# Sorting the eighth pair of heads as well: its rows ranked and scattered while early pairs are computed

## The chip, the cores and the metric

The kernel runs on one core of one Trainium2 chip. Its engines are TensorE (PE in the profile, with its weight loads as PEld), VectorE (DVE), ScalarE (ACT), GpSimd (POOL) and SyncE (SP, which here only starts DMA transfers). Each works through its own list of instructions in order and waits where another engine's or a transfer's result is needed. The metric is the device time in microseconds; lower is better.

## The reference

Two blocks, one after the other. Attention has 4 batches of 8 heads, 768 tokens, 64 dimensions; a query sees only keys of its own cluster (one of 16 per head, by the largest product with unit centroids). The result, heads side by side, goes through a feed-forward block 512 to 2048 to 512 with a hard-swish between.

```python
q_assign = np.argmax(np.einsum('bhsd,hcd->bhsc', q_n, c_n), axis=-1)
k_assign = np.argmax(np.einsum('bhsd,hcd->bhsc', k_n, c_n), axis=-1)
mask = q_assign[:, :, :, None] == k_assign[:, :, None, :]
scores = scale * np.matmul(q, k.transpose(0, 1, 3, 2))
scores = np.where(mask, scores, -1000000000.0)
attn = softmax(scores)            # written out in the reference
x = attn @ v                      # (B,H,S,D) -> (B*S, H*D) = 3072 x 512
h = x @ w_in                      # 512 x 2048
g = h * np.clip(h + 3.0, 0.0, 6.0) / 6.0
out = g @ w_out                   # 2048 x 512
```

The two weight matrices come as doubles and are turned into floats inside the kernel.

## The kernel before

Heads are taken in 16 pairs; four pairs make a batch. `FIRST` (8) divides them.

**Early stage, pairs 0 to 7, dense.** A loop over `n` takes key tiles of 128, twelve for each pair (two halves of the queries times six key tiles), two per turn of the loop; here such a turn is called an iteration, and `r` is `n` modulo 12. For each key tile `scores` (L407) makes, for both heads, 128 keys x 384 queries in PSUM tile `ps` (two buffers): once with the vectors (`xf`), once with one-hot clusters (`xm`), which adds a huge negative number where clusters differ. `exponentials` (L430, ACT) writes `ex` (six buffers). `key_sums` (L437 for the first sum of a half, L440 for the four after it, all on POOL) adds the tiles up in `acc`. `attn_v` (L450) multiplies by the values, two key tiles later. After a pair, `sum_up` (L476, `pd`) sums over the partitions. Between these, the next pair is prepared: `turn` (L325), `cluster_scores` (L344), `route` (L355, with a maximum and two comparisons on DVE), `route_turn` (L386). Its steps lie at r = 0, 2, 4, 6, 8, 10.

In the same loop the weights are decoded: 32 chunks, five steps each. `split` is an absolute sum on ACT (L235) and a shift on DVE (L239), `join` is on DVE (L245), `power` is a Relu sum on ACT with the constant `w_low` as its bias (L251) and a mask on DVE (L255), `rest` (L261) and `total` (L266) are on DVE. Four steps for sums of weights follow, so there are 164 in all. `share(n, r)` says how many of these run at the end of each iteration. From n = 60 on, at the eight places `up_at`, one item of the feed-forward block of batch 0 is worked in: `ph` (L634), a `lift` on ACT, a `clip` on DVE (L520) and, after every second item, four `gated_sums` (L676) on POOL. `sooner` says at which of them a set of `kept_sums` (L576) of weights is made.

**Late stage, pairs 8 to 15, sorted.** For each pair the kernel finds every row's position when rows are sorted by cluster: `own_clusters`, `run_up`, `step_up`, `order` (`rk`, L1048 and L1061), `positions`. `scatter` writes the rows of q and of k with v to DRAM in that order, 24 indirect DMAs from POOL (L1094). After each one, `pause` writes the constant `w_low` three times (L1086). `load_ranked` reads the rows back, `turn_ranked` transposes them (L978), `band_masks`, `band_scores` (L1139) and `band_values` (L1196) work on bands of at most 352 queries for 128 keys instead of on all 768, `band_sums`, `band_divide` (L1233, L1237) and `keep_ranked` finish the rows, `gather` (L1109) fetches them back in their first order, `turn_back` transposes them.

What runs where in this stage is written out by hand: `steps_of(g)` lists steps with an offset, `late_plan` puts the step of pair `g` at plan point `AHEAD + SLOT * (g - FIRST) + offset` (38 and 28), and each point also pops one item of the feed-forward list `fill`, except two points in each slot. A token block (256 tokens, three in a batch) has eight `up` items and seven `down` items, of two parts each. The first block is done as written; in the other eleven, products are formed by a scheme with seven half-size products and sums instead of eight (L686, L725).

**Order.** The whole is under a manual schedule: the instruction lists are in the order in which the program emits them, and waits come from which tile an instruction reads or writes.

Of the kernel before, what the change touches and what calls it, by code (L numbers as in the profile page):

```python
# [46 lines left out]
FIRST = NPAIR // 2  # L47
# [75 lines left out]
def fast_path(ctx, tc, ok, q, k, v, centroids, moe_w_in, moe_w_out, out):  # L123
# [49 lines left out]
    plain = const.tile([P, FIRST // NKT, 2 * NKT * NCH], F32, name="plain")  # L173
# [7 lines left out]
    later = []  # L181

# [8 lines left out]
    def load(g, *names):  # L191
        if g > FIRST or (g == FIRST and "v" in names):
            return
        b, h = divmod(2 * g, H)
        for name in names:
            if name == "v":
                dst = st["v", g] = vp.tile([P, 2, NCH, D], F32, name="vt")
            elif name == "q":
                if g == 1:
                    spare = g_sb.rearrange("p k i c -> p (k i c)")[:, 0 : NC2 * P]  # L200
                    st["qk", g] = spare.rearrange("p (a j t d) -> p a j t d", a=2, j=NCH, t=2)
                else:
                    st["qk", g] = qkp.tile([P, 2, NCH, 2, D], F32, name="qk")
# [111 lines left out]
    def turn(g, part, bank=None, held=None):  # L315
        if part == 0:
            st["xf", g] = xp.tile([P, NC2, P], F32, name="xf")
# [22 lines left out]
    def cluster_scores(g):  # L340
# [7 lines left out]
        cs = st["cs", g] = st.get("rankp", rtp).tile([P, NC2 // 4, P], F32, name="cs", tag="third")  # L348
# [83 lines left out]
    def key_sums(n):  # L432
        g, hf, j = where(n)
        ex = st["ex", n]
        if j == 1:
            acc = st["acc", g, hf] = accp.tile([P, 2, HALF], F32, name="acc")
            nc.gpsimd.tensor_tensor(out=acc, in0=st["ex", n - 1], in1=ex, op=ALU.add)  # L437
# [29 lines left out]
    def sum_up(g):  # L467
        b, kt = divmod(g, NKT)
        if kt == 0:
            for name in ("sums", "rd"):  # L470
                st[name, b] = dram.tile([NKT, 2, S], F32, name=f"{name}{b}")
# [12 lines left out]
        if kt == NKT - 1:  # L484
            load_sums(b)

    def load_sums(b):
        tok = plain[:, b]
# [7 lines left out]
        def complete():  # L496
            waiting.extend((b, m) for m in range(NHC))
            load_block()
# [8 lines left out]
    def divide(b, m):  # L507
        if ("rb", b, m) in st:
            xb, rb = st["xb", b, m], st.pop(("rb", b, m))
            nc.vector.tensor_tensor(out=xb, in0=xb, in1=rb, op=ALU.mult)  # L510
# [39 lines left out]
    def load_block():  # L550
        if waiting and st["free"]:
# [5 lines left out]
            if ("rd", b) in st:  # L557
                rb = st["rb", b, m] = xbp.tile([P, NKT, 2 * P], F32, name="rb", tag="xs")
                for t in range(2):
                    nc.sync.dma_start(  # L560
                        rb[t * D : (t + 1) * D], st["rd", b][:, t, part].unsqueeze(0).to_broadcast([D, NKT, 2 * P])
# [51 lines left out]
    def ffn_items(b):  # L613
        def up(m, i):
# [11 lines left out]
            def end():  # L626
                if u < HF:
                    if u in sooner:
                        kept_sums(sooner[u], nc.vector if u % 2 else nc.gpsimd)
# [185 lines left out]
    def whether_good():  # L815
        good = smallp.tile([P, 2, FIRST * 2 * NCH], F32, name="good", tag="sane")
        flat = plain.rearrange("p b n -> p (b n)")
        for a, (bound, op) in enumerate(((BOUND, ALU.is_le), (1.0 / BOUND, ALU.is_ge))):
            nc.vector.tensor_scalar(out=good[:, a], in0=flat, scalar1=bound, scalar2=None, op0=op)
# [65 lines left out]

    def open_late():
# [11 lines left out]
        for a, i in enumerate((1, NCH - 2)):  # L898
# [3 lines left out]
        rankp = st["rankp"]  # L902
# [6 lines left out]
        places = st["places"] = rankp.tile([P, S], mybir.dt.int16, name="places")  # L909
# [6 lines left out]
        st["before"] = rankp.tile([P, P], BF16, name="before")  # L916
        nc.gpsimd.memset(st["before"], 0.0)
        nc.gpsimd.affine_select(
            out=st["before"], in_=st["before"], compare_op=ALU.is_ge, fill=1.0, base=0,
            pattern=[[-1, P]], channel_multiplier=1,  # L920
        )
        st["every"] = rankp.tile([P, P], BF16, name="every")
        nc.gpsimd.memset(st["every"], 1.0)
        st["runs"] = rankp.tile([P, 2, NCH, 2, C], BF16, name="runs")
        nc.gpsimd.memset(st["runs"], 0.0)
        st["steps"] = rankp.tile([P, 3, 2, 2, C // 2 + C], BF16, name="steps")
        nc.gpsimd.memset(st["steps"], 0.0)
        st["upto"] = rankp.tile([P, 2, C // 2 + 2 * D], BF16, name="upto")
        nc.gpsimd.memset(st["upto"], 0.0)
# [62 lines left out]
    def own_clusters(g):  # L992
# [9 lines left out]
        if g == FIRST:  # L1002
# [37 lines left out]
    def order(g):  # L1040
        rankp = st["rankp"]
# [23 lines left out]
        prod = rankp.tile([P, 2 * NC2, C], F32, name="prod", tag="third")  # L1065
# [6 lines left out]
    def positions(g):  # L1072
        prod = st.pop(("prod", g))
        posf = st["rankp"].tile([P, 2 * NC2], F32, name="posf", tag="mx")
        nc.vector.reduce_sum(out=posf, in_=prod, axis=AX.X)
        pos = st["pos", g] = st["posp"].tile([P, 2, NCH, 2], I32, name="pos")
# [11 lines left out]
    def scatter(g, a):  # L1088
        pos = st["pos", g]
        src, name = (st.pop(("kvn", g)), "kvd") if a else (st.pop(("qn", g)), "qd")  # L1090
        for t in range(2):
            done = []
            for j in range(NCH):
# [8 lines left out]
                pause()  # L1102

# [168 lines left out]
    def steps_of(g):  # L1272

        first, last = g == FIRST, g == NPAIR - 1
        f = -3 if first else -5
        if first:
            plan = [
                (-38, load_queries), (-37, load_keys, 0), (-36, load_keys, 1), (-37, run_up),
                (-36, step_up), (-31, order), (-30, positions), (-20, lambda g: st.pop("signed")()),
            ]  # L1280
        else:
# [6 lines left out]
        plan += [  # L1288
            (s, scatter, 0), (s, scatter, 1), (-12, band_masks), (-11, load_ranked, 0), (f, load_ranked, 1),
            (f + 1, load_ranked, 2), (-1, turn_ranked, 0), (0, turn_ranked, 1),  # L1290
        ]
# [10 lines left out]
    def late_plan():  # L1302

        at = {}
        for g in range(FIRST, NPAIR):
            for _, offset, op, *args in steps_of(g):
                i = AHEAD + SLOT * (g - FIRST) + offset
# [6 lines left out]
    def prep_items(g, r):  # L1314

        if g > FIRST:
            return []
        turns = [lambda part=part: turn(g, part) for part in range(3)]
        if g == FIRST:
# [22 lines left out]
    sooner = {0: 7, 2: 6, 3: 3, 4: 5, 6: 4}  # L1342
    up_at = (60, 64, 70, 72, 82, 84, 90, 94)
    READY, DECODED = per_batch + 2 * lag_d, 2 * per_batch

    def share(n, r):


        if n < READY:
            return {0: 4, 2: 3, 4: 3, 6: 1, 8: 2, 10: 4}[r]  # L1350
        if n < DECODED - 2 * per_pair:
            return {0: 6, 2: 5, 4: 4, 6: 3, 8: 5, 10: 5}[r]
        if n < DECODED - per_pair:
            return {0: 8, 2: 3, 4: 3, 6: 2, 8: 4, 10: 8}[r]
        return {0: 6, 2: 5, 4: 4, 6: 1, 8: 3, 10: 4}[r]
# [18 lines left out]
    with tc.manual_schedule():  # L1374
# [24 lines left out]
        for n in range(0, total + lag_d + 2, 2):  # L1399
# [11 lines left out]
            if m >= 0 and m % per_pair == per_pair - 1:  # L1411
                sum_up(m // per_pair)
                ready(m)
            if prep and r == 4:
# [9 lines left out]
            for step in prep:  # L1424
                step()
# [395 lines left out]
```

## Time and profile before

| | us |
|---|---|
| median of 3 runs (933.91 to 934.87) | 934.68 |
| the profiled execution, its own time | 934.64 |
| its span | 932.8 |
| TensorE busy | 917.6 |
| VectorE busy | 554.7 |
| ScalarE busy | 334.4 |
| GpSimd busy | 584.4 |

The granted TensorE clock was 0.998 of full speed. Times in the profile count from the start of the span. A group of instructions is shown as line, engine, operation, the tile written and the tiles read, their shapes and the count; after it the busy time in us, the mean of one in ns, and the idle time of its engine just before, with what ended it. A row of a timeline is the start in us, how long it lasted, engine, line and operation; what stands in square brackets is the idle time before it and what ended it. A row of the windows view is the stretch, its length, then for each engine its busy time with the count, then the TensorE clock, the share in which the DMA engines were busy and GB/s.

### The profile page before, as it was taken

Reading aid. Unit: us, or ns where it says so; the run is one execution under the profiler, and the core shown is the slowest. Engines: PE = TensorE matmul, PEld = TensorE weight load, DVE = VectorE, ACT = ScalarE, POOL = GpSimd, SP = SyncE. Lnnn points to the kernel's source line nnn. Section 1 sums busy time; section 2 is a strip of 40 time slices with the busy share of each in tenths; the row PEclk is TensorE's granted clock in tenths of the full one; section 3 lists DMA queues with packets and bytes.
Section 4 is the critical chain, followed back from the end, with each engine's and each line's share of the span. In section 5 each row is a group of like instructions: output and inputs, shape, how many; then the busy total and the mean of one; then the engine's idle time right before and its main releaser. Section 6 shows DMA issues by size and latency. Waiting matters only on the chain.

```text
span 932.8 us, 17534 instructions
## 1 busy us (share of the span) xinstructions
PE 917.6 (98%) x6350; PEld 720.4 (77%) x6350; DVE 554.7 (59%) x1299; ACT 334.4 (36%) x667; POOL 584.4 (63%) x1313
## 2 busy tenths in 40 slices
PE   8999999999999999999999999999999999999997
PEld 5444445555898798897887988988888899999996
DVE  6667667878875484493483572673571655536361
ACT  6888877774022332232232241331422311112120
POOL 3877878779285887877788787777876061203030
PEclk9999999999999999999999999999999999999999
DMA  8454576441466466583682835655463324323220
GB/s 199 135 131 129 144 198 182 135 143 62 108 192 175 124 187 145 146 211 81 190 201 77 230 90 156 175 159 128 132 173 83 103 69 130 91 74 108 59 67 27
DMA packets 177023, 124.77 MB, mean 134 GB/s; under 512 B 135680, under 2 KB 155168, under 8 KB 176928
## 3 DMA queue, kind: packets, MB, share of 16 engines
q1 hardware_dynamic: 153968, 76.52, 31.4%
q10 hardware_dynamic: 13744, 34.44, 12.8%
q0 software_dynamic: 9216, 12.60, 4.2%
q8 instruction: 52, 0.85, 0.4%
q14 instruction: 43, 0.35, 0.1%
HBM read 95.11 MB, written 28.41 MB: 132 GB/s over the span
## 4 chain that ended last, share of the span: by engine, by line
PE 93%; ACT 2%; DMA 2%; DVE 1%; issue 1%; SPq 1%; DVEq 0%; ACTq 0%
PE Y L725 18%; PE uY L686 17%; PE X L725 14%; PE uX L686 13%; PE ps L407 7%; PE pv L450 6%; PE ph L634 3%; PE pv L1196 3%; PE ps L978 3%; PE ps L1139 2%; PE pcs L344 1%; PE pv L1139 1%; PE pqk L325 1%; DMA rb<-rd 1%; PE pd L476 1%
## 5 line engine op out<-in xcount | busy, mean ns | idle before, releaser
L440 POOL TENSOR_TENSOR acc<-acc,ex 128x768 f32<-128x768 f32 x64 | 124.4, 1944 | 25.3 <-ACT ex L430 21.9
L1094 POOL DMA_INDIRECT qd<-qn,pos x96 | 97.7, 1018 | 44.1 <-DVE tx L576 17.9
L1109 POOL DMA_INDIRECT xn<-xsd,pos x96 | 93.3, 972 | 50.9 <-DVE g_sb L676 29.2
L676 POOL TENSOR_TENSOR g_sb<-g_sb 128x256 f32<-128x256 f32 x52 | 39.2, 774 | 121.8 <-DVE g_sb L520 120.8
L517 ACT ACTIVATE sx<-g_sb,half_c 128x512 f32<-128x512 f32 x88 | 63.6, 723 | 143.3 <-DVE g_sb L697 129.6
L1086 POOL MEMSET w_low<- 128x1 f32 x864 | 90.9, 105 | 33.3
L1094 POOL DMA_INDIRECT kvd<-kvn,pos x96 | 96.1, 1001 | 22.1 <-issue 22.1
L732 DVE TENSOR_TENSOR y<-y,Y 128x256 f32<-128x256 f32 x47 | 19.8, 421 | 128.3 <-PE Y L725 118.7
L686 PE MATMUL uX<-xb,w_in_sb 128*128 128x128 f32 x704 | 93.0, 275 | 0.0
L725 PE MATMUL X<-w_out_sb,g_sb 128*128 128x256 f32 x384 | 90.3, 382 | 0.0
L725 PE MATMUL Y<-T,g_sb 128*128 128x256 f32 x384 | 88.0, 381 | 0.0
L725 PE MATMUL Y<-w_out_sb,g_sb 128*128 128x256 f32 x384 | 87.7, 380 | 0.0
L686 PEld LDWEIGHTS uX<-xb,w_in_sb 128*128 128x128 f32 x704 | 85.7, 192 | 0.0
L725 PEld LDWEIGHTS Y<-T,g_sb 128*128 128x128 f32 x384 | 72.1, 190 | 13.0 <-issue 3.3
L725 PEld LDWEIGHTS X<-w_out_sb,g_sb 128*128 128x128 f32 x384 | 71.0, 190 | 13.8 <-issue 4.0
L725 PEld LDWEIGHTS Y<-w_out_sb,g_sb 128*128 128x128 f32 x384 | 71.8, 190 | 10.5 <-issue 1.0
L697 DVE TENSOR_TENSOR sx<-uX,sx 128x128 f32<-128x128 f32 x176 | 51.1, 290 | 47.8 <-ACT sx L704 35.3
L407 PE MATMUL ps<-xf 64*128 64x384 f32 x384 | 78.5, 487 | 0.3 <-ACT ex L430 0.3
L430 ACT ACTIVATE ex<-ps 128x768 f32<-128x768 f32 x96 | 72.9, 802 | 5.9 <-PE ps L407 5.8
L450 PE MATMUL pv<-ex,vt 128*64 128x384 f32 x384 | 72.5, 499 | 0.0
L697 DVE TENSOR_TENSOR g_sb<-uY,sx 128x128 f32<-128x128 f32 (+1 forms) x176 | 65.6, 414 | 0.0
L520 DVE SCALAR_TENSOR_TENSOR g_sb<-sx,g_sb 128x512 f32<-128x512 f32 x88 | 63.7, 726 | 2.5 <-ACT sx L517 2.5
(211 smaller groups left out, 1726.1 us busy)
## 6 DMA issues: line engine op xcount, KB each, us to landing
tx<-td ACTq DMA_DIRECT2D x86, 384.0 KB
raw<-in_moe_w_in_dram SPq DMA_DIRECT2D x16, 512.0 KB
raw<-in_moe_w_out_dram SPq DMA_DIRECT2D x16, 512.0 KB
xb<-xd SPq DMA_DIRECT2D x12, 512.0 KB
out_dram<-y SPq DMA_DIRECT2D x44, 128.0 KB
qk<-in_k_dram SPq DMA_DIRECT2D x16, 192.0 KB
vt<-in_v_dram SPq DMA_DIRECT2D x16, 192.0 KB
xd<-num SPq DMA_DIRECT2D x16, 192.0 KB
```

Source lines behind the costliest of these rows:

```text
L407: nc.tensor.matmul(st["ps", n][:, t, 0:HALF], lhsT=x[r, NCH + j], rhs=x[r, hf * NHC : (hf + 1) * NHC], start=first, stop=last, skip_group_ ...
L430: nc.scalar.activation(out=ex, in_=sc, func=ACT.Exp, scale=SM_SCALE)
L440: nc.gpsimd.tensor_tensor(out=acc, in0=acc, in1=ex, op=ALU.add)
L450: nc.tensor.matmul(pv[t * D : (t + 1) * D], lhsT=vt[:, t, j], rhs=ex[:, t], start=(j == 0), stop=(j == NCH - 1),)
L517: nc.scalar.activation(out=r, in_=h, func=ACT.Relu, bias=half_c, scale=1.0 / 6.0)
L520: nc.vector.scalar_tensor_tensor(out=g, in0=r, scalar=1.0, in1=h, op0=ALU.min, op1=ALU.mult)
L686: nc.tensor.matmul(dst, lhsT=w[:, kt], rhs=x(kt), start=(kt == 0), stop=(kt == HK - 1))
L697: nc.vector.tensor_tensor(out=out_, in0=in0, in1=in1, op=ALU.add)
L725: nc.tensor.matmul(bank[:, half * HC : (half + 1) * HC], lhsT=g_sb[:, kind, i], rhs=w[:, i], start=(first and i == 0), stop=(last and i == ...
L1086: nc.gpsimd.memset(w_low, W_LOW)
L1094: i = nc.gpsimd.indirect_dma_start(out=rows[name, g, t], in_=src[:, j, t].rearrange("p a d -> p (a d)") if a else src[:, j, t], in_offset= ...
L1109: nc.gpsimd.indirect_dma_start(out=xn[:, j, t], out_offset=None, in_=rows["xsd", g, t], in_offset=bass.IndirectOffsetOnAxis(ap=pos[:, 0, j ...
```

## The change

`FIRST` becomes 7, and `SECOND` is 8. Pairs 0 to 6 stay dense, and pair 7 joins the sorted ones. Because its place in the plan lies one slot ahead of pair 8, whose steps start with the late stage, its ranking is put into the early stage and the rest into plan points 1 to 47:

- `ranking`: queries and keys are loaded at n = 8 into free space in `g_sb`, turned at n = 18 to 22; helper constants are set at 30, cluster scores at 32, own clusters at 34, `run_up` and `step_up` at 36, `order` and `positions` at 40.
- `early_rows` fetches rows of q, then of k with v, in six parts (at n = 36, 40, 52, 62, 68, 74) into the two buffers `sx`.
- `early_scatter` writes them, 24 indirect DMAs from POOL, in the iterations of n = 42 to 82 (`WRITING`), after the iteration's sums over keys: one for each iteration, two at n = 42, 48 and 54. Each is followed by `pause`.
- In that stretch, as long as n < 60, the first sum over keys of a half is made on DVE rather than on POOL.
- All 164 decoding steps now fit in 84 key tiles: 20 for a pair up to n = 36, 23 up to 60, 29 after.
- `kept_sums` runs on DVE alone, four sets ahead of time rather than five; `up_at` moves to 60, 64, 70, 72, 76, 80, 82, 84.
- Batch 1 has three pairs that need dividing by sums (`unsorted`), and its feed-forward items arrive when pair 7 comes back rather than at the end of the early stage.

```diff
-FIRST = NPAIR // 2
+FIRST = NPAIR // 2 - 1
+SECOND = FIRST + 1
...
+    spare = g_sb.rearrange("p k i c -> p (k i c)")
...
         if j == 1:
             acc = st["acc", g, hf] = accp.tile([P, 2, HALF], F32, name="acc")
-            nc.gpsimd.tensor_tensor(out=acc, in0=st["ex", n - 1], in1=ex, op=ALU.add)
+            eng = nc.vector if WRITING[0] <= n < up_at[0] else nc.gpsimd
+            eng.tensor_tensor(out=acc, in0=st["ex", n - 1], in1=ex, op=ALU.add)
...
-        if kt == NKT - 1:
+        if kt == unsorted(b) - 1:
             load_sums(b)
+    def unsorted(b):
+        return min(FIRST - NKT * b, NKT)
...
-                        kept_sums(sooner[u], nc.vector if u % 2 else nc.gpsimd)
+                        kept_sums(sooner[u], nc.vector)
...
+    def early_rows(n):
+        b, h = divmod(2 * FIRST, H)
+        src = sxp.tile([P, 4, P], F32, name="sx").rearrange("p k c -> p (k c)")
+        if n < 2:
+            src = src[:, 0 : NCH * D].rearrange("p (j d) -> p j d", j=NCH)
+            nc.sync.dma_start(src, q[b, h + n].rearrange("(p j) d -> p j d", p=P))
+        else:
+            t, part = divmod(n - 2, 2)
+            js = slice(part * NHC, (part + 1) * NHC)
+            src = src[:, 0 : NHC * 2 * D].rearrange("p (j a d) -> p j a d", j=NHC, a=2)
+            for a, x in enumerate((k, v)):
+                nc.sync.dma_start(src[:, :, a], x[b, h + t].rearrange("(p j) d -> p j d", p=P)[:, js])
+        st["rows", n] = src
+
+    def early_scatter(i):
+        a, r = divmod(i, 2 * NCH)
+        t, j = divmod(r, NCH)
+        src = st["rows", i // NHC - 2][:, j % NHC] if a else st["rows", t][:, j]
+        done = st.setdefault(("done", a, t), [])
+        one = nc.gpsimd.indirect_dma_start(
+            out=rows["kvd" if a else "qd", FIRST, t], in_=src.rearrange("p a d -> p (a d)") if a else src,
+            in_offset=None,
+            out_offset=bass.IndirectOffsetOnAxis(ap=st["pos", FIRST][:, a, j, t : t + 1], axis=0),
+        )
+        for other in done:
+            tc.declare_no_dep(one.ins, other.ins, reason="rows of one permutation")
+        done.append(one)
...
-        first, last = g == FIRST, g == NPAIR - 1
+        first, last = g == SECOND, g == NPAIR - 1
...
+        elif g == FIRST:
+            plan = [(-7, lambda g: st.pop("signed")())]
...
+        if g == FIRST:
+            plan += [(-9, load_ranked, 0), (-6, load_ranked, 1), (-5, load_ranked, 2), (-6, band_masks)]
...
-                i = AHEAD + SLOT * (g - FIRST) + offset
+                i = AHEAD + SLOT * (g - SECOND) + offset
...
-    sooner = {0: 7, 2: 6, 3: 3, 4: 5, 6: 4}
-    up_at = (60, 64, 70, 72, 82, 84, 90, 94)
+    sooner = {0: 7, 2: 6, 4: 5, 6: 4}
+    up_at = (60, 64, 70, 72, 76, 80, 82, 84)
+    WRITING = (42, 84)
...
+        if n < 36:
+            return {0: 4, 2: 4, 4: 4, 6: 1, 8: 3, 10: 4}[r]
+        if n < 60:
+            return {0: 5, 2: 4, 4: 4, 6: 2, 8: 4, 10: 4}[r]
+        if n < 72:
+            return {0: 6, 2: 5, 4: 4, 6: 3, 8: 5, 10: 6}[r]
+        return {0: 6, 2: 6, 4: 5, 6: 2, 8: 5, 10: 5}[r]
...
+    ranking = {
+        8: [load_first], 18: [lambda: turn(FIRST, 0)], 20: [lambda: turn(FIRST, 1)], 22: [lambda: turn(FIRST, 2)],
+        30: [helpers], 32: [lambda: cluster_scores(FIRST)], 34: [lambda: own_clusters(FIRST)],
+        36: [lambda: run_up(FIRST), lambda: step_up(FIRST)], 40: [lambda: order(FIRST), lambda: positions(FIRST)],
+    }
+    for n, part in ((36, 0), (40, 1), (52, 2), (62, 3), (68, 4), (74, 5)):
+        ranking.setdefault(n, []).append(lambda part=part: early_rows(part))
+    writes = [lambda i=i: early_scatter(i) for i in range(4 * NCH)]
...
             if m >= 0 and m % per_pair == per_pair - 1:
                 sum_up(m // per_pair)
                 ready(m)
+            if WRITING[0] <= n < WRITING[1]:
+                for _ in range(2 if n < up_at[0] and n % NCH == 0 else 1):
+                    writes.pop(0)()
+                    pause()
...
             for step in prep:
                 step()
+            for step in ranking.get(n, []):
+                step()
```

## The prediction

> **What bounds the kernel now.** I read the page's busy times first, then the two early stretches of the windows view, then the early stage in order of time, one engine at a time.
>
> ```profile
> PE 917.6 (98%) x6350; PEld 720.4 (77%) x6350; DVE 554.7 (59%) x1299; ACT 334.4 (36%) x667; POOL 584.4 (63%) x1313
> 20.00:120.00 100.00, 99.72 (x688) 43.18 (x688) 67.14 (x85) 80.74 (x164) 81.60 (x44) 1.00 0.53 142
> 120.00:232.00 112.00, 110.13 (x682) 58.90 (x678) 88.73 (x108) 76.04 (x155) 88.92 (x60) 1.00 0.47 139
> 232.00:260.00 28.00, 28.00 (x151) 24.81 (x149) 22.76 (x53) 1.49 (x4) 9.39 (x20) 1.00 0.51 141
> ```
>
> The windows columns are span, PE, PEld, DVE, ACT, POOL, clock, DMA share, GB/s. TensorE is busy 99.72 of 100 us in the early stage and in all of 232 to 260, so only TensorE work removed, or a TensorE wait added, moves the end. But early ACT and POOL are each some 81% busy: there they have about a fifth to spare, against 63% for POOL over the whole span.
>
> **Part 1: TensorE work, dense against sorted.** The rows are windows of single lines (PE, then PEld): L407 scores, L450 values and L386 mask transposes in the early stage (8 dense pairs); then, for the 8 sorted pairs, L1139 band scores, L1196 band values, L978 transposes (one sorted turn is 12 of 222), L1233 and L1237 dividing, L1061 ranks.
>
> ```profile
> 0.00:240.00 240.00, 88.11 (x576) 39.26 (x576) 1.00 0.53 145
> 0.00:240.00 240.00, 72.53 (x384) 23.28 (x384) 1.00 0.53 145
> 0.00:240.00 240.00, 7.94 (x96) 5.56 (x96) 1.00 0.53 145
> 240.00:760.00 520.00, 36.15 (x288) 18.40 (x288) 1.00 0.55 148
> 240.00:760.00 520.00, 29.02 (x256) 16.95 (x256) 1.00 0.55 148
> 240.00:760.00 520.00, 30.56 (x222) 25.70 (x222) 1.00 0.55 148
> sum 933.00, PE 3.93 PEld 3.02; mean PE 0.98 PEld 0.75
> sum 933.00, PE 6.55 PEld 5.49; mean PE 1.64 PEld 1.37
> sum 933.00, PE 5.43 PEld 3.69; mean PE 1.36 PEld 0.92
> ```
>
> Removed with the dense pair: (88.11 + 72.53 + 7.94)/8 = 21.1 us. Added with the sorted one: 36.15/8 + 29.02/8 = 8.1, 18 transposes at 30.56/222 = 2.5, (3.93 + 6.55 + 5.43)/8 = 2.0, and some 0.2 for the four small rank matmuls: 12.8 us. The key sum over all partitions, the turns, cluster scores and arg-max transposes occur either way. Net -8.2 us. It is bounded by 0, were the band work to meet waits as long as itself, and by -8.2; I take -8.2, because 232 to 260 and its neighbours run TensorE at 28.00 of 28.
>
> **Part 2: the 24 scatters between the key sums.** Here is the early stage in order of time: TensorE, then ACT, then POOL, then two iterations on POOL with a `ph` between; last, rows of POOL's scatters as they run late now, and two successive `pd` (one per pair).
>
> ```profile
> 97.35 0.34 PE L407 MATMUL ps<-xm 64*128 64x384 bf16 x2
> 100.95 0.34 PE L407 MATMUL ps<-xm 64*128 64x384 bf16 x2
> 101.12 0.81 PE L407 MATMUL ps<-xf 64*128 64x384 f32 x4
> 104.55 0.92 PE L407 MATMUL ps<-xf 64*128 64x384 f32 x4
> ...
> 98.44 1.62 ACT L430 ACTIVATE ex<-ps 128x768 f32<-128x768 f32 x2 [0.98 <-PE ps L407]
> 101.76 0.71 ACT L251 ACTIVATE wsize<-wsize,w_low 128x512 bf16<-128x512 bf16 x1
> 102.47 0.35 ACT L373 ACTIVATE seen<-one_hot 128x192 bf16<-128x192 bf16 x1
> 103.30 1.49 ACT L430 ACTIVATE ex<-ps 128x768 f32<-128x768 f32 x2
> 105.37 0.68 ACT L235 ACTIVATE wsize<-raw 128x512 bf16<-128x512 f32 x1
> 106.18 0.72 ACT L251 ACTIVATE wsize<-wsize,w_low 128x512 bf16<-128x512 bf16 x1
> ...
> 99.39 4.05 POOL L440 TENSOR_TENSOR acc<-acc,ex 128x768 f32<-128x768 f32 x2 [1.10 <-ACT ex L430]
> 145.48 4.04 POOL L440 TENSOR_TENSOR acc<-acc,ex 128x768 f32<-128x768 f32 x2 [0.39 <-ACT ex L430]
> 151.62 3.36 POOL L676 TENSOR_TENSOR g_sb<-g_sb 128x256 f32<-128x256 f32 x4 [2.10 <-DVE g_sb L520]
> ...
> 260.87 0.96 POOL L1094 DMA_INDIRECT qd<-qn,pos  x1 [0.15 <-issue]
> 261.82 0.42 POOL L1086 MEMSET w_low<- 128x1 f32 x3
> 262.40 0.96 POOL L1094 DMA_INDIRECT qd<-qn,pos  x1 [0.16 <-issue]
> ...
> 64.56 0.85 PE L476 MATMUL pd<-acc,ones 128*32 128x384 f32 x8
> 88.39 0.85 PE L476 MATMUL pd<-acc,ones 128*32 128x384 f32 x8
> 146.37 3.72 PE L634 MATMUL ph<-xb,w_in_sb 128*128 128x256 f32 x16
> ```
> ```profile
> L440 POOL TENSOR_TENSOR acc<-acc,ex 128x768 f32<-128x768 f32 x64 | 124.4, 1944 | 25.3 <-ACT ex L430 21.9
> L430 ACT ACTIVATE ex<-ps 128x768 f32<-128x768 f32 x96 | 72.9, 802 | 5.9 <-PE ps L407 5.8
> L440 POOL TENSOR_TENSOR acc<-acc,ex x64: 1802/1822/2689, 18.3 to 228.7; 128x768 f32<-128x768 f32 x64
> ```
>
> An iteration is two key tiles. On TensorE it takes 3.6 us where little preparation falls in (97.35 to 100.95 to 104.55); a pair of six takes 88.39 - 64.56 = 23.8, so the three that hold the turns, `pd` and cluster scores (r = 0, 2, 4) mean (23.8 - 10.8)/3 = 4.3. A `ph` adds 3.7.
>
> A scatter with its pause is 262.40 - 260.87 = 1.53 us of POOL. The pause is three memsets of `w_low`, and `w_low` is also the bias of the decode step `power` on ACT (the L251 rows). Nothing writes it early today. In the changed kernel's order of instructions every one of the 17 `power` steps from n = 44 on gets a wait on POOL, for the last memset of its own iteration. ACT works its list in order, and behind that `power` stand the next two exponentials. So a loop closes: exponentials, two sums on POOL, scatter, memsets, `power`, next exponentials. Its length: POOL starts 0.95 after the exponentials start (98.44 to 99.39); two sums 2 x 1.944; the gap of 0.16 and scatter 0.96 with memsets 0.42; 0.1 to ACT, and `power` 0.72 to the next exponential (106.18 to 106.90, where ACT starts it). Together 7.2 us against 3.6. What stands behind `power` and ahead of the exponentials comes on top: a `split` 0.9 (105.37, with its accumulator read), or two `seen` 0.9.
>
> TensorE has some slack: with `ps` double buffered, the exponentials due at 102.0 need only end by 104.55, when TensorE wants their bank; they last 0.8, so 1.7 us, given back once after each late stretch. Iteration by iteration, lateness against TensorE's own pace:
>
> - n = 44: 7.2 + 0.9 - 3.6 = 4.6. 46: 3.6. 48 has no POOL sum (its first sum goes to DVE) and two scatters, 3.3 in all: back 1.0.
> - 50 has no `power`, so POOL falls behind; 52 waits for both: 6.4 + 5.5 + 0.1 + 0.7 + split 0.9 = 13.6 against 8.6: 5.0. 54, again two scatters, done while `split` runs: back 1.3.
> - 56 (no `power`) and 58: 13.6 - 7.2 = 6.4. 60 holds a `ph` (7.3 or more, as long as the loop): back 1.7.
> - 62: 7.2 + 0.9 - 4.3 = 3.8. 64 (`ph`): back 1.7.
> - 66: POOL still runs the gated sums of `ph` 64. They start after the clip, 151.62 against sums from 145.48, and end some 3.1 into 66: 3.1 + 1.9 + 1.5 + 0.8 - 3.6 = 3.7. 68: 4.6. 70: back 1.7.
> - 74, likewise behind gated sums: 3.1 + 3.9 + 1.5 + 0.9 + 0.9 - 4.3 = 6.0. 76: back 1.7. 78 (one sum): 6.0 - 3.6 = 2.4. 80: back 1.7. 82 has no `power`.
>
> Total +29.3 us. Bounds: with sums at their median of 1.82 us and all 1.7 given back each time, and nothing standing behind `power`, about +19; with sums at 2.5, as they run below beside DVE's largest operations, about 9 loops x 1.1 more: +40.
>
> ```profile
> 221.29 10.08 POOL L440 TENSOR_TENSOR acc<-acc,ex 128x768 f32<-128x768 f32 x4 [0.73 <-ACT ex L430]
> L510 DVE TENSOR_TENSOR xb<-xb,rb 128x1024 f32<-128x1024 f32 x1 | 2.6, 2633 | 3.4 <-DMA rb<-rd 3.4
> 249.21 1.22 DVE L510 TENSOR_TENSOR xb<-xb,rb 128x1024 f32<-128x1024 f32 x1
> L261 DVE SCALAR_TENSOR_TENSOR wunit<-raw,wunit 128x512 f32<-128x512 uint32 x32 | 44.4, 1388 | 1.1
> L245 DVE SCALAR_TENSOR_TENSOR wtop<-raw,wtop 128x512 uint32<-128x512 uint32 x32 | 22.3, 698 | 1.0
> ```
>
> **Part 3: the rest.** Decoding in seven pairs: a step is (1.388 + 4 x 0.698)/5 = 0.84 us of DVE; 23 steps instead of 17 per pair for n = 36 to 60 add 5.0 to 67% of 23.8 = 16.0, with a first sum twice (a product of 128x1024 takes DVE 1.22 to 2.63, so 128x768 some 0.9 to 2.0, say 1.4) 23.8: DVE would be full at TensorE's old pace. I cost it at 0, since the loop of part 2 stretches that very window by half; without that cover I price it at up to 4. The first scatter waits for pair 7's positions on that DVE: 0 to 3, taken 0. `kept_sums` goes from POOL to DVE, three operations a set; one set (1.3 us) lands in 232 to 260, with band masks and the sign step, into 5.2 idle us of DVE: 0 to 3, taken 0. The ten row loads on SP (two `vt` loads go) sit in a DMA share of 0.53, and each row tile is fetched at least four key tiles ahead: 0, or 2 if SP's list, which carries the raw weights too, blocks on a row tile not yet written out. Late, pair 7 adds nine loads and stores on SP and 12 gathers (18 us of POOL at 1.53), which fall between the scatters of pairs 8 and 9, at a time when POOL now idles 18.6 of 28; its band work and return take one slot as each other pair's do, under block 1's items; batch 1's items arrive at plan point 47, with batch 0's still in hand: 0.
>
> **Sum.** The profiled execution took 934.64 (median of the runs 934.68). 934.6 - 8.2 + 29.3 = 955.7, say 956.
>
> **Rivals.**
> - *The POOL work fits and only part 1 is left* (the other side): ACT must get its memset before TensorE needs the bank, 3.6 + 1.7 = 5.3 after the exponentials begin, so two sums must cost under 2.0 together. Against: 4.05 in both quoted rows. For: POOL idles a fifth of the early stage. 926 to 931.
> - *Only POOL's throughput counts*: were ACT not held, n = 42 to 60 gives POOL 12 sums and 12 scatters, 41.7 us, against 34.6 of TensorE; six `ex` buffers hold most of that lag. Price 0 to 7 over part 1, plus DVE's 4: 927 to 938.
> - *TensorE slows as well.* Today no gap of it in the early stage is long, and the clock is 1.00 in all rows. The loop leaves gaps of 3.6 to 5. If the clock halved behind them, the part of a `ph` iteration just after a gap would stretch, about 1.7 each: 7 x 1.7 = +12, 968, up to 980. The Trainium skill (TensorE: Matmul & The Clock Gate, the section on the HAM clock gate) says that a window of about 3.4 us without activity halves the clock until a busy one; no run here shows it.
>
> **How the numbers follow.** ACT-POOL loop as summed, 0.65 (own range 945 to 968); fits, 0.11; throughput only, 0.10; clock too, 0.10; another cause, such as a load or a late wait worth over 15, 0.04. Range 934 to 970: outside are the first rival, half the second's low end, half the clock's. A measurement here tells 0.2% (1.9 us). Faster 0.15 (first rival, part of the second), same 0.03, slower 0.82.
>
> **What would show it.** ACT's idle time before `power` released by POOL's memset, from the first scatter until decoding ends; TensorE under 80% busy in that stretch and over 98% after; the last key sum near 237 instead of 228.7; the late stage 12 to 13 us longer. Wrong if `power` waits for nothing while TensorE stays full (then 927), if POOL's sums are long done when the memsets come, or if most lost time lies past the early stage.

## The result and the profile after

The changed kernel takes 955.4 us (median; 954.83 to 956.51) against 934.21 for the kernel before beside it. By the means of the six runs of each it is 1.0231 times as long, 95% interval 1.0218 to 1.0244, or 21.6 us. The profiled execution has a span of 954.7 us and a mean clock of 0.99.

First the page's busy times after the change, then its windows (span, PE, PEld, DVE, ACT, POOL, clock, DMA share, GB/s), in stretches cut at the first scatter and at the last sums over keys.

```profile
PE 920.3 (96%) x6323; PEld 725.0 (76%) x6323; DVE 554.9 (58%) x1341; ACT 328.9 (34%) x659; POOL 597.8 (63%) x1438
20.00:100.00 80.00, 79.94 (x564) 35.75 (x562) 57.63 (x86) 69.17 (x145) 64.69 (x40) 1.00 0.59 160
100.00:240.00 140.00, 115.57 (x668) 60.51 (x665) 88.66 (x129) 74.92 (x157) 100.78 (x136) 0.94 0.42 126
240.00:270.00 30.00, 29.60 (x156) 24.75 (x156) 28.27 (x62) 3.51 (x6) 10.03 (x20) 1.00 0.67 179
```

Up to 100 us TensorE is as full as before. From 100 to 240 TensorE is busy 115.57 of 140 us, no engine is full, and the clock is 0.94. That is the stretch of the 24 scatters; behind it TensorE is full again. That no engine is full points to a loop of waits. The view of ACT's waits and that of tile `acc` (shortest, median and longest of one in ns, then first and last start) say which:

```profile
ACT wsize L260 <- POOL w_low L1129: 50.6, 15, 6.4
L456 POOL TENSOR_TENSOR acc<-acc,ex x56: 1796/1820/2182, 19.7 to 238.1; 128x768 f32<-128x768 f32 x56
```

ACT's decode step `power` (L260 now) waited 15 times for POOL's memset of `w_low`, 50.6 us in all; before, no such row existed. The last sum over keys starts at 238.1 instead of 228.7. (Of these 9.4 us 1.4 lie ahead of the loop: the first sum of that row starts at 19.7 instead of 18.3. That belongs to this execution and not to the change, for in runs 7, 8 and 10, with the same work there, it starts at 18.0 to 18.4.) From it to the end of the span it is 954.7 - 238.1 = 716.6 us, before 932.8 - 228.7 = 704.1: the late stage is 12.5 longer.

One turn of the loop, ACT first and then POOL, in order of time:

```profile
112.73 1.49 ACT L445 ACTIVATE ex<-ps 128x768 f32<-128x768 f32 x2
...
118.89 0.72 ACT L260 ACTIVATE wsize<-wsize,w_low 128x512 bf16<-128x512 bf16 x1 [3.33 <-POOL w_low L1129]
...
119.61 0.79 ACT L445 ACTIVATE ex<-ps 128x768 f32<-128x768 f32 x1
```
```profile
113.60 3.68 POOL L456 TENSOR_TENSOR acc<-acc,ex 128x768 f32<-128x768 f32 x2 [2.46 <-ACT ex L445]
117.44 0.98 POOL L1166 DMA_INDIRECT qd<-sx,pos  x1 [0.16 <-issue]
118.44 0.42 POOL L1129 MEMSET w_low<- 128x1 f32 x3
```

Exponentials at 112.73, sums at 113.60, scatter at 117.44, memsets until 118.86, `power` at 118.89, the next exponentials at 119.61: 6.88 us from exponentials to exponentials. Each step starts when the one before ends, the sums when the first of the two exponentials does.

### The profile page after: what moved, and what is told of

Its sections match the earlier page's. It is cut to its first block, busy times and chain, and to the rows that moved or that the text cites. A ratio compares the mean times of both kernels' runs of the same rounds, so it can differ in the third digit from the quotient of the medians.

```text
span 954.7 us, 17658 instructions
## 1 busy us (share of the span) xinstructions
PE 920.3 (96%) x6323; PEld 725.0 (76%) x6323; DVE 554.9 (58%) x1341; ACT 328.9 (34%) x659; POOL 597.8 (63%) x1438
## 4 chain that ended last, share of the span: by engine, by line
PE 80%; POOL 7%; DVE 5%; ACT 3%; issue 2%; DMA 1%; ACTq 0%; POOLq 0%; DVEq 0%
PE Y L748 18%; PE uY L709 16%; PE X L748 13%; PE uX L709 12%; POOL acc L456 4%; PE ps L422 3%; PE pv L1267 3%; PE pv L466 3%; PE ps L1019 3%; PE ps L1210 3%; PE pv L1210 1%; ACT ex L445 1%; PE pcs L355 1%; POOL kvd L1166 1%; PE pqk L336 1%
## 5 line engine op out<-in xcount | busy, mean ns | idle before, releaser
L1180 POOL DMA_INDIRECT xn<-xsd,pos x108 | 107.1, 992 | 50.6 <-ACT sx L539 26.1
L456 POOL TENSOR_TENSOR acc<-acc,ex 128x768 f32<-128x768 f32 x56 | 105.2, 1878 | 38.1 <-ACT ex L445 35.4
L1129 POOL MEMSET w_low<- 128x1 f32 x972 | 102.1, 105 | 37.6
L1137 POOL DMA_INDIRECT kvd<-kvn,pos x96 | 96.0, 1000 | 21.6 <-issue 21.6
L422 PE MATMUL ps<-xf 64*128 64x384 f32 x336 | 73.5, 516 | 3.7 <-ACT ex L445 3.7
L466 PE MATMUL pv<-ex,vt 128*64 128x384 f32 x336 | 65.8, 514 | 0.0
L445 ACT ACTIVATE ex<-ps 128x768 f32<-128x768 f32 x84 | 63.3, 799 | 2.4 <-PE ps L422 2.0
```

Of the source, the lines that this page charges most:

```text
L422: nc.tensor.matmul(st["ps", n][:, t, 0:HALF], lhsT=x[r, NCH + j], rhs=x[r, hf * NHC : (hf + 1) * NHC], start=first, stop=last, skip_group_ ...
L445: nc.scalar.activation(out=ex, in_=sc, func=ACT.Exp, scale=SM_SCALE)
L456: nc.gpsimd.tensor_tensor(out=acc, in0=acc, in1=ex, op=ALU.add)
L466: nc.tensor.matmul(pv[t * D : (t + 1) * D], lhsT=vt[:, t, j], rhs=ex[:, t], start=(j == 0), stop=(j == NCH - 1),)
L1129: nc.gpsimd.memset(w_low, W_LOW)
L1137: i = nc.gpsimd.indirect_dma_start(out=rows[name, g, t], in_=src[:, j, t].rearrange("p a d -> p (a d)") if a else src[:, j, t], in_offset= ...
```

## The experiments

All are compared with the kernel before on the chip on which they ran; ratios, not times, go across.

| what is altered | us | before beside it | ratio (95%) |
|---|---|---|---|
| the change itself | 955.4 | 934.21 | 1.0231 (1.0218 to 1.0244) |
| 1: after, pauses on an own tile | 931.33 | 932.31 | 0.999 (0.998 to 0.9999) |
| 2: as 1, one memset instead of three | 933.3 | 932.31 | 1.0005 (0.9994 to 1.0017) |
| 3: before, with pauses on `w_low` | 942.84 | 932.31 | 1.0112 (1.0095 to 1.0129) |
| 4: before, with pauses on an own tile | 932.41 | 932.31 | 1.0002 (0.9992 to 1.0012) |
| 5: as 1, first feed-forward item later | 926.89 | 931.89 | 0.9944 (0.993 to 0.9957) |
| 6: as 5, scatters begin later | 933.84 | 931.89 | 1.0016 (1.0007 to 1.0025) |
| 7: after, six memsets of `w_low` | 961.14 | 931.89 | 1.0313 (1.0297 to 1.0328) |
| 8: after, TensorE's gaps filled | 953.21 | 931.89 | 1.0221 (1.0205 to 1.0236) |
| 9: as 5, positions earlier | 929.51 | 932.14 | 0.9965 (0.995 to 0.9979) |
| 10: after, first feed-forward item later | 954.26 | 932.14 | 1.0236 (1.022 to 1.0252) |
| 11: as 9, POOL relieved twice | 930.04 | 938.88 | 0.9904 (0.9876 to 0.9932) |
| 12: as 9, one memset instead of three | 929.62 | 938.88 | 0.9903 (0.9868 to 0.9937) |

The theory: `power` waits for the pause's memset because both touch `w_low`, and this closes a loop between ACT and POOL. The main rival: it is POOL's added time. Others: a full VectorE, a late load, the lower clock.

**1 and 2. The wait taken away, the work kept.**

```diff
+    pausing = const.tile([P, 1], F32, name="pausing")
...
     def pause():
         for _ in range(PAUSE):
-            nc.gpsimd.memset(w_low, W_LOW)
+            nc.gpsimd.memset(pausing, W_LOW)
```

> The changed kernel, with the memsets of the pauses writing a tile of their own instead of `w_low`; everything else, the 24 scatters on POOL too, is as changed. Theory (the decode step `power` waits for the memsets, and closes the loop between ACT and POOL): the waits of `power` on POOL are gone, and most of part 2 with them: 934.6 - 8.2 = 926.4, and up to 11 more where POOL's sums and scatters alone are more than TensorE's pace (41.7 against 34.6 us in n = 42 to 60) and for DVE: about 931, range 926 to 938; last key sum at about 212 us instead of 238. Rival, POOL's time by itself (scatters take 0.98 us each in front of sums, and the exponentials wait for free buffers): 945 to 955, with ACT waiting for POOL at the exponentials. Rival, DVE full with the first sums and the denser decoding: 940 or more, with DVE over 95% busy between 102 and 160.

Run 2 has `pause(1)` behind the early scatters besides.

> As the run with a tile of its own, and one memset instead of three behind each early scatter. It takes 24 x 0.28 = 6.7 us off POOL between 102 and 212. Theory: POOL is then only near its limit in n = 42 to 60, so that 0 to 4 us less than with three memsets: 926 to 931. If POOL's time by itself is the bound, the whole 6.7 us come off. If DVE or the clock holds the stretch, no difference.

Run 1 took 0.999 of the kernel before: 2.4% of 934, some 22.5 us of the change's time, hung on which tile a memset writes, while the scatters, the memsets and all sums stayed where they were. That excludes POOL's added time as the cause of these 22.5 us. But the 8 us that the sorted pair saves did not appear either. I had expected about 931, and so it came, but the wait that cost TensorE most was not on POOL or VectorE, as I had it, but on a load. Run 1 on TensorE and on VectorE:

```profile
106.11 0.51 PE L402 MATMUL po<-ident_q,one_hot 128*128 128x128 bf16 x6 [1.67 <-DVE one_hot L380]
143.04 6.74 PE L658 MATMUL ph<-xb,w_in_sb 128*128 128x256 f32 x16 [4.07 <-DVE xb L533]
```
```profile
140.64 2.25 DVE L533 TENSOR_TENSOR xb<-xb,rb 128x1024 f32<-128x1024 f32 x1 [6.87 <-DMA rb<-rd]
```

The first `ph` waited 4.07 us for the product of `xb` and `rb`, which waited 6.87 us for the load of `rb`; and behind that gap the `ph` took 6.74 us instead of 3.72. Run 2 missed what I expected (931.33 less 0 to 4): it came out no faster. Its rows show why:

```profile
144.80 5.13 PE L658 MATMUL ph<-xb,w_in_sb 128*128 128x256 f32 x16 [6.95 <-DVE xb L533]
```
```profile
141.63 3.01 DVE L533 TENSOR_TENSOR xb<-xb,rb 128x1024 f32<-128x1024 f32 x1 [7.81 <-DMA rb<-rd]
```

The load came no sooner than in run 1, so all that POOL gained ahead of it went into a longer wait.

**3 and 4. The wait alone, with no sorting.** The kernel before, with a pause in each iteration and no scatter.

```diff
                 sum_up(m // per_pair)
                 ready(m)
+            if 42 <= n < 84:
+                pause()
```

> The kernel before, nothing sorted early, with one pause (three memsets of `w_low`) after the sums of each iteration from n = 42 to 82: 21 x 0.42 = 8.8 us of POOL, no scatters. Theory: the 15 `power` steps in that stretch wait for POOL, and the loop is 0.95 + 2 x 1.82 + 0.16 + 0.42 + 0.1 + 0.72 = 6.0 us long where TensorE needs 3.6 to 4.3 (7.3 with a `ph`): 9 iterations without a `ph` lose about 2 each, less what the slack of 1.7 gives back: 12 to 18 us slower than before, 946 to 953. Rival, only POOL's time counts: it idles a fifth of this stretch, so 0 to 1 us slower.

> The same pauses in the kernel before, but on a tile of their own that nothing reads. Theory: nothing waits for them, 8.8 us of POOL fit in its idle time: 934 to 936. Rival, POOL's time or the memsets as such: as slow as with `w_low`.

On `w_low` the 21 pauses cost 10.5 us (1.0112), on a tile that nothing reads nothing at all (1.0002). So 8.8 us of POOL work are free, and the wait is not. I had expected 12 to 18. The view of ACT's waits in run 3 shows the size:

```profile
ACT wsize L251 <- POOL w_low L1086: 24.3, 11, 3.3
```

Eleven of the fifteen `power` steps waited, 2.2 us on average; the short gaps between them may give TensorE's slack back more often than I counted, but no run shows that.

**5 and 6. What was left.**

```diff
-                later.append(lambda: divide(0, 0))
+                later.append(lambda: later.append(lambda: divide(0, 0)))
...
-    up_at = (60, 64, 70, 72, 76, 80, 82, 84)
+    up_at = (62, 64, 70, 72, 76, 80, 82, 84)
```

(The two places that used `up_at[0]` keep 60.) Run 6 has `WRITING = (44, 88)` besides.

> The kernel with a tile of its own for the pauses, and two moves: the first feed-forward item at n = 62 instead of 60, and the product of `xb` and `rb` that it needs one iteration later. That run lost 4.07 us of TensorE to this product, which waited 6.87 us for its load, and its `ph` then took 6.74 us instead of 3.72. If the load and the lower clock behind the gap are what is left of the loss: 4.1 + 3.0 = 7 us off its 931.3, so 924 to 927, faster than before. If the load is only waited for elsewhere: 929 to 932.

> As the run with the late product, and scatters from n = 44 to 86 instead of 42 to 82, so that the first no longer waits for pair 7's positions, and the first sum of n = 43 stays on POOL. If the waits on a full VectorE around 102 to 112 (1.67 + 0.34 + 0.49 us of TensorE in the run with a tile of its own) come from this: 2 to 3 us less than the run with the late product. If decoding alone fills VectorE there: no difference.

Run 5 is 0.9944 of the kernel before, some 5 us faster, and inside the 924 to 927 expected. Of the 7 us that run 1 had lost to the load and the clock some 4 came off (0.999 to 0.9944). TensorE in it: the `ph` no longer waits and takes its 3.72 us again, but ahead of it `pd` now waits 1.66 us for POOL's sums.

```profile
105.04 0.51 PE L402 MATMUL po<-ident_q,one_hot 128*128 128x128 bf16 x6 [1.68 <-DVE one_hot L380]
109.49 0.92 PE L423 MATMUL ps<-xf 64*128 64x384 f32 x4 [0.34 <-ACT ex L446]
110.89 0.50 PE L423 MATMUL ps<-xm 64*128 64x384 bf16 x4 [0.49 <-ACT xm L407]
143.91 0.85 PE L493 MATMUL pd<-acc,ones 128*32 128x384 f32 x6 [1.66 <-POOL acc L457]
144.69 3.72 PE L658 MATMUL ph<-xb,w_in_sb 128*128 128x256 f32 x16
```

Run 6 missed: it lost 7 us more. SP's issue of the same row tile in run 5; then, in run 6, that issue and the later one of `rb`, the scatter from that tile's buffer, and the product:

```profile
122.26 0.39 SPq L1159 DMA_DIRECT2D sx<-in_k_dram  x1
```
```profile
130.88 0.39 SPq L1159 DMA_DIRECT2D sx<-in_k_dram  x1
138.25 1.30 SPq L583 DMA_DIRECT2D rb<-rd  x2
```
```profile
128.11 1.52 POOL L1167 DMA_INDIRECT qd<-sx,pos  x1 [0.15 <-issue]
```
```profile
146.91 1.22 DVE L533 TENSOR_TENSOR xb<-xb,rb 128x1024 f32<-128x1024 f32 x1 [9.87 <-DMA rb<-rd]
```

The row tile asked for at n = 52 needs the buffer that the first six scatters read. With the scatters begun one iteration later, the sixth moved from n = 48 to n = 52 itself, where it started at 128.11. SP works its list in order, so it stood still until 130.88, 8.6 us later than in run 5, and the loads of `qk`, `vt`, `xb` and `rb` stood behind it.

Run 6 did answer the question that it was made for: the waits near 105 stayed (1.61, 0.32 and 0.49 us), so the start of the scatters does not cause them. The first of them:

```profile
105.04 0.51 PE L402 MATMUL po<-ident_q,one_hot 128*128 128x128 bf16 x6 [1.61 <-DVE one_hot L380]
```

**7. The wait made longer.** After, with `pause(6)` behind each early scatter.

> The changed kernel with six memsets of `w_low` instead of three behind each early scatter: 0.42 us more of POOL in an iteration. Theory of the loop through `power`: each of some 14 iterations that are bound by it gets 0.42 us longer (three with two scatters twice that): 955 + 5 to 8, 960 to 963. If the change's loss were fixed waits (positions, a load, the clock) and not the loop: 955 to 957.

1.0313 against 1.0231: 0.82%, or 7.6 us, for 24 x 0.42 = 10.1 us more of POOL; inside the 5 to 8 expected of the loop. ACT's waits for it grew with it:

```profile
ACT wsize L260 <- POOL w_low L1129: 57.6, 15, 7.1
```

**8. The clock.** After, with TensorE's four long gaps filled.

```diff
+            filler = {48: 14, 56: 24, 68: 18, 80: 18}.get(n, 0)
+            if filler:
+                idle_bank = scratch([P, P], "filler")
+                for _ in range(filler):
+                    nc.tensor.matmul(idle_bank, lhsT=ident, rhs=ident, start=True, stop=True)
             for i in steps:
                 scores(i)
```

> The changed kernel, with small products of the identity with itself (14, 24, 18, 18 of 128x128, never read) put ahead of the scores of n = 48, 56, 68 and 80, where TensorE idled 3.15, 5.52, 4.10 and 4.08 us and its next 2 to 5 us then ran at half speed; at 0.165 us each they fill all but 1 to 1.5 us of each gap. If the lower clock behind the gaps is part of the loss and on the path: some 2 us back at each, 945 to 949. If the loop through POOL alone sets the pace and the slow products are covered by it: 954 to 957.

The stretch from 100 to 240 in this run, ACT's wait, and the sums over keys:

```profile
100.00:240.00 140.00, 129.21 (x816) 76.59 (x815) 90.02 (x130) 75.26 (x157) 102.89 (x136) 0.98 0.43 129
```
```profile
ACT wsize L260 <- POOL w_low L1129: 50.2, 15, 5.8
L456 POOL TENSOR_TENSOR acc<-acc,ex x56: 1802/1820/2668, 18.3 to 237.4; 128x768 f32<-128x768 f32 x56
```

The clock rose from 0.94 to 0.98, and the time stayed: 1.0221 against 1.0231, with ACT waiting 50.2 instead of 50.6 us, and 219.1 us from the first sum to the last instead of 218.4. Most of the slow stretches were repaired, and nothing clear of the spread came back (the two intervals leave room for some 3 us). The filling was not clean: the products took 0.23 us each instead of 0.165, so at n = 56 and 68 they held the scores back by some 1.3 us. At n = 48 and 80 they held nothing back, and there the next exponentials followed at the same distance as in the changed kernel: 6.90 us against 6.88 from n = 46 to 48, and 5.87 in both from n = 78 to 80. So in the changed kernel the low clock lies beside the loop, not in it. (In run 1, where no loop covers it, the same thing cost the `ph` 3.0 us.)

**9, 11 and 12. The waits that are left.** Run 9:

```diff
-            eng = nc.vector if WRITING[0] <= n < 60 else nc.gpsimd
+            eng = nc.vector if 48 <= n < 60 else nc.gpsimd
...
-        36: [lambda: run_up(FIRST), lambda: step_up(FIRST)], 40: [lambda: order(FIRST), lambda: positions(FIRST)],
+        36: [lambda: run_up(FIRST), lambda: step_up(FIRST)], 38: [lambda: order(FIRST), lambda: positions(FIRST)],
```

> The kernel with the tile of its own and the late product; besides, pair 7's `order` and `positions` at n = 38 instead of 40, and the first sum of n = 43 on POOL instead of VectorE. In that kernel the first scatter waited 2.2 us for the positions, and TensorE lost 1.68 + 0.34 + 0.49 us between 103 and 111 to a VectorE busy 9.66 of 10. If the order and the one sum are the cause: 2 to 3 us less, 924 to 925. If decoding alone fills VectorE: no difference. The row tiles are asked for at the same iterations, so that no load should be later.

The waits near 105 went from 2.5 to 0.8 us as expected, but the time did not follow (0.9965 against 0.9944), for a larger wait came, on TensorE:

```profile
107.53 0.92 PE L423 MATMUL ps<-xf 64*128 64x384 f32 x4 [0.33 <-ACT ex L446]
108.93 0.50 PE L423 MATMUL ps<-xm 64*128 64x384 bf16 x4 [0.49 <-ACT xm L407]
145.91 1.50 PE L493 MATMUL pd<-acc,ones 128*32 128x384 f32 x6 [5.62 <-POOL acc L457]
```

From 100 to 152 POOL idles no longer than 0.2 us at a time, and `pd` waits for its sums: here its time does bound. POOL is as full in runs 1 and 5 from 106 on; in run 5 that showed as the 1.66 us of `pd`. Runs 11 and 12 take time off it: one memset behind each early scatter in both, and in 11 the first sum of n = 43 back on VectorE.

> As the run with early positions, but POOL relieved: one memset instead of three behind each early scatter (13 of them before n = 62: 3.6 us), and the first sum of n = 43 on VectorE again (1.82 us). In the run with early positions POOL had no idle time but 0.16 us between instructions from 100 to 152, and `pd` waited 5.62 us for its sums. If POOL's time is now what bounds: 5.4 of the 5.62 us and the slow stretch behind it go, and what early positions gave stays: 922 to 925, less than the 926.9 of the run with the late product. If the positions' move itself costs, or VectorE does again: 927 to 930.

> As the run with early positions, with one memset instead of three behind each early scatter and the first sum of n = 43 left on POOL. If POOL's time bounds: 3.6 of the 5.62 us go, and TensorE's slow stretch with them: 924 to 927. If not: 929 to 930.

On the chip of these two the kernel before itself varied from 934.43 to 942.12, so they show 0.990 with wide intervals and can't be ranked against run 5. The times expected (922 to 925 and 924 to 927) both missed, but they had been worked out from runs on another chip. Their traces do say what happened: the wait of `pd` is gone in both, and the `ph` waits for the load of `rb` once more (run 11, then run 12).

```profile
144.18 5.38 PE L658 MATMUL ph<-xb,w_in_sb 128*128 128x256 f32 x16 [2.93 <-DVE xb L533]
```
```profile
144.96 5.38 PE L658 MATMUL ph<-xb,w_in_sb 128*128 128x256 f32 x16 [3.17 <-DVE xb L533]
```

**10. One fix without the other.** After, with `w_low` still written, and only the later item of run 5.

> The changed kernel with `w_low` still written by the pauses, and only the first feed-forward item and its product moved later (62 instead of 60). If the loop through `power` covers the load that the product waits for, as in the changed kernel's trace (1.39 us of VectorE instead of 6.87), the move brings nothing: 952 to 957. If the two losses simply add up, 7 us off: 946 to 949.

1.0236, no gain: the loop had covered that load. The two losses don't add up, each hides the other. Against run 5, from which it differs only in the tile that the memsets write, it prices the loop: 1.0236 - 0.9944 = 2.92%, 27.2 us (some 2 either way by the two intervals).

Runs 5, 9, 11 and 12 are faster than both kernels, by 1% of the kernel before at most. The best that is clear of the spread is run 5, 0.9944.

## Why the prediction was right, step by step

- **Part 1 (-8.2): about right.** In run 5, where little hides it, TensorE's busy time, on the page of that run, is 7.5 us under that of the kernel before (917.6). The kernel's time falls by some 5 only. The waits in run 5's rows, 1.68 + 0.34 + 0.49 us on VectorE and 1.66 on POOL, are large enough for the difference; that they are the whole of it is not shown.

```profile
PE 910.1 (98%) x6323; PEld 720.4 (78%) x6323; DVE 558.0 (60%) x1341; ACT 329.7 (36%) x659; POOL 602.5 (65%) x1438
```

- **Part 2 (+29.3): mechanism right, size some 2 too high.** The loop measures 27.2, some 2 either way (run 10 against run 5). One turn was put at 7.2 and measures 6.88: 0.87 to the sums, 3.84 with the gap behind them, 1.00 to the memsets and 0.42 for them, 0.03 and 0.72. Of the 17 `power` steps that were to wait, 15 did. Runs 1, 3, 4 and 7 each show that it is the wait and not the work.
- **The list by iteration** is right as a whole more than step by step. The nine stretches that it lets the loop bind (n = 44, 46, 50 and 52, 56 and 58, 62, 66, 68, 74, 78) add up to 82.5 us from exponentials to exponentials, and measure 81.9 in the changed kernel. But single ones are off, by 1.4 too long to 2.0 too short: n = 50 and 52 took 13.39 of 13.6, n = 56 and 58 14.94 of 13.6, n = 74 8.94 of 10.3. ACT's rows that bound the first two:

```profile
123.93 1.49 ACT L445 ACTIVATE ex<-ps 128x768 f32<-128x768 f32 x2
...
137.32 1.49 ACT L445 ACTIVATE ex<-ps 128x768 f32<-128x768 f32 x2
...
139.97 0.81 ACT L445 ACTIVATE ex<-ps 128x768 f32<-128x768 f32 x1
...
154.91 1.49 ACT L445 ACTIVATE ex<-ps 128x768 f32<-128x768 f32 x2
```

  And at n = 64, 70, 76 and 80, where the list lets TensorE win 1.7 back, `power` still waited for the memset, 4.00, 2.77, 4.00 and 1.29 us. (The two terms written as 4.6 are 4.5 by their own parts, 7.2 + 0.9 - 3.6.)
- **The largest miss in the list** is its first step: from n = 44 to 46 the exponentials move from 102.51 to 112.73 in the changed kernel's trace, 10.2 us, where 3.6 + 4.6 = 8.2 were planned. The first scatter had waited for pair 7's positions, and behind the scatters the sums waited for the first sum, which VectorE now makes (ACT's and POOL's rows):

```profile
102.51 1.62 ACT L445 ACTIVATE ex<-ps 128x768 f32<-128x768 f32 x2 [0.98 <-PE ps L422]
```
```profile
102.04 1.14 POOL L1166 DMA_INDIRECT qd<-sx,pos  x1 [2.19 <-DVE pos L1120]
...
105.54 4.02 POOL L456 TENSOR_TENSOR acc<-acc,ex 128x768 f32<-128x768 f32 x2 [0.37 <-DVE acc L453]
```

  The first is the term "0 to 3, taken 0"; 2 would have been right. But earlier positions alone would not have saved it: in run 11 the positions come early, and the sums still waited 2.14 us for VectorE's first sum. VectorE was late for both.
- **Part 3, VectorE (taken 0, up to 4 uncovered):** right uncovered, where it costs TensorE 1.68 + 0.34 + 0.49 = 2.5 us in run 5. In the changed kernel it was not quite 0: it is the 2 us of the step above.
- **Part 3, SP (0, or 2 if its list blocks on a row tile): the upper bound was too low.** The list did not block in the changed kernel, but run 6 shows that two iterations less between the last scatter from a buffer and the next request for it make it block, for 8.6 us of SP and 7 us of the kernel. The loads behind a blocked issue wait as well, and one of them was the next to be late.
- **What the prediction did not have:** the load of `rb`. It named the cover (the loop stretches that window) for VectorE but did not ask what TensorE would next wait for, were the loop gone. It would have been `xb` times `rb`: 4.07 us and 3.0 of slow `ph`.
- **The rival "only POOL's throughput"** gave 927 to 938 for a kernel whose ACT is not held. Run 1 lies there, and TensorE's largest wait in it was the load. POOL's own limit costs TensorE 1.66 us in run 5 and 5.62 in run 9.
- **The rival "TensorE slows as well"** came true as a fact and not as a price. The clock was 0.94 from 100 to 240, which is 140 x 0.06 = 8.4 us of TensorE at full speed, but run 8 got nothing clear of the spread back for most of it; the 1.7 us for each `ph` is in no run. Of the rule in the Trainium skill (TensorE: Matmul & The Clock Gate, the section on the HAM clock gate), that after an idle window of some 3.4 us TensorE runs at half speed until a busy one, the half speed agrees: the granted clock is 0.50 from 113.60 to 115.60 us in the changed kernel. The idle window does not, in the cases of the last section.
- **The late stage** was put at 12 to 13 us longer and is 12.5, counted from the last sum over keys. In the changed kernel one `ph` of 3.72 us stands behind that sum, and in the kernel before none. Counted from the first product `X` of the feed-forward block, which stands behind every `ph` in both, it is 11.3 longer (954.7 - 242.76 = 711.9 against 932.8 - 232.21 = 700.6). Before, then after:

```profile
232.21 1.99 PE L725 MATMUL X<-w_out_sb,g_sb 128*128 128x256 f32 x8
```
```profile
242.76 1.99 PE L748 MATMUL X<-w_out_sb,g_sb 128*128 128x256 f32 x8
```

- **The other signs.** TensorE was to be under 80% busy in the stretch and over 98% behind it; it is 83% busy from 100 to 240, part of it at the low clock, and 98.7% behind. The last sum was to start near 237 and did at 238.1, 1.4 of it the late start of that execution.
- **The sum was luckier than its terms.** It gave 955.7 to 956, and 955.4 came. With the load out of the way, parts 1 and 3 together bring 5 and not 8 (run 5), and the loop costs 27 and not 29 (run 10 against run 5): two misses of 2 to 3 us that cancel. The loop itself, its place and its price are not luck.

## What to carry to other kernels

A write that changes no value is still a write: before an instruction is added as padding, look up who reads its tile, and on which engine, or give it a tile that nobody reads. When no engine is full and one wait repeats with the length of a whole round trip, look for a loop of waits through in-order engines, and test it by cutting the wait and leaving the work. And when a loss is removed, ask what is late next: here a load that came no sooner, then a full VectorE, then a full POOL stood behind it, hardly visible while the loop covered them.

## What the runs showed of the hardware

TensorE's clock fell after gaps shorter than I had thought, and not by the length of one gap alone. Single gaps of 1.66 to 1.82 us left it at full speed (the `ph` of run 5 is right behind one of 1.66; the one of 1.82 is in run 3, ahead of 190.53 us). One of 3.15 us halved it at once (the changed kernel), and in run 3 one of 1.97 us, which came some 4 us behind one of 0.56, halved it 0.8 us after the restart: the granted clock is 0.50 from 127.4 to 130.5 us. First the row of the changed kernel, then those of run 3:

```profile
113.57 1.65 PE L422 MATMUL ps<-xf 64*128 64x384 f32 x4 [3.15 <-ACT ex L445]
```
```profile
126.47 0.34 PE L407 MATMUL ps<-xm 64*128 64x384 bf16 x2 [1.97 <-ACT ex L430]
126.63 0.92 PE L407 MATMUL ps<-xf 64*128 64x384 f32 x4
127.31 0.56 PE L407 MATMUL ps<-xm 64*128 64x384 bf16 x2
127.63 1.52 PE L407 MATMUL ps<-xf 64*128 64x384 f32 x4
```

In run 7 two shorter gaps did it, 0.98 and 1.07 us, with 0.92 us of products between them: the scores behind them took 1.49 us instead of 0.81. In the changed kernel the gaps at the same place were 0.51 and 1.06 us (ahead of 191.62 and 193.60 us), and the scores behind them took their 0.81 us. Run 7:

```profile
195.23 0.92 PE L422 MATMUL ps<-xf 64*128 64x384 f32 x4 [0.98 <-ACT ex L445]
197.22 0.63 PE L422 MATMUL ps<-xm 64*128 64x384 bf16 x4 [1.07 <-ACT xm L406]
197.64 1.49 PE L422 MATMUL ps<-xf 64*128 64x384 f32 x4
```

Whether it goes by a sum or by where a gap falls in a window of its own was not tried.
